# A linear-attention layer with a two-matrix feed-forward: wider idle products, and the last output tile copied and sent by columns

## The chip, the cores and the metric

One of the cores of a Trainium2 chip runs the whole program. The metric is the device time in microseconds (us) of one execution; lower is better. The engines are TensorE (PE, its weight loads shown apart as PEld), VectorE (DVE), ScalarE (ACT), GpSimd (POOL) and SyncE (SP). SP and ACT issue the DMAs; their issuing instructions are shown as SPq and ACTq, and their DMAs appear as queue q1 (SP) and q10 (ACT).

## What is computed

```python
def _attn_ref(r, k, v, w, u):                # all (4, 8, 768, 48), u (8, 48)
    for t in range(S):
        cur = np.einsum('bhd,bhe->bhde', u[None] * kt, vt)
        y[:, :, t] = np.einsum('bhd,bhde->bhe', rt, state + cur)
        state = wt[:, :, :, None] * state + np.einsum('bhd,bhe->bhde', kt, vt)

def _moe_ref(x, w_in, w_out, alpha):          # x (3072, 384), w_in (384, 2048), w_out (2048, 384)
    h = x @ w_in
    g = np.maximum(h, 0.0) + alpha * np.minimum(h, 0.0)
    return (g @ w_out).astype(np.float32)
```

The output of the attention, laid out as 3072 tokens of 384 features, is the `x` of the second function. Everything is float32.

## The kernel before

**Tiles and groups.** Time is cut into chunks of 64 steps; a chunk of two batches is one attention tile of 128 partitions (`q`, 24 of them). Three such tiles are one group `g` of 384 tokens (`GS = 3`, `GT = 384`; eight groups). For each group the feed-forward runs over 16 slices of the hidden size (`j`): `moe_up` makes 128 hidden features of 384 tokens in a PSUM bank (L684), ACT and DVE apply the slope (L689, L691) and split the result in two float32r parts (L695, L696), and `moe_down` adds the products with `w_out` to three PSUM tiles `op0` to `op2` (L709), one for each 128 tokens. Group 0 works on plain float32 (`wf`, `pos`); later groups on pairs of float32r parts. `moe_out` copies `op0` to `op2` to SBUF and sends them to the output.

**What sets the order.** All work is first written as operations of a planner (`Plan`), with an engine, a planned duration, what it reads and writes, and a due time; a simulated run of the plan puts them in order, and the program is emitted in that order. Each engine executes its own list in order. The plan's numbers are not times of the chip.

**Idle products of PE.** `warm()` is a 128x128 block of the constant 1e-18 that POOL sets at the start (L315, in a tile of the ring `os`). PE first runs `MADE = 12` products of that block with itself (`wm`, L738), into a PSUM bank that nobody reads. While the program is emitted, wherever the plan leaves PE idle for more than `FILL_MIN`, before the first use of `op2`, further such products are put in (L834), as many as fit at `FILL = 0.24` us each, into `op2`. There are 17 of them, in seven places: 2, 3, 3, 3, 2, 1 and 3. A plain float32 product shows as two MATMUL records and two weight loads in the trace. So L738 has 24 records and L834 has 34.

**The last output.** In the last group ACT copies `op0` (L726) and DVE copies `op1` and `op2` (L723), 384 columns each. Every tile holds 64 rows of each of two batches, and goes out in two DMAs (L731) of 64 partitions by 384 columns (1,536 bytes a row): in the last group the first half of the partitions is issued by SP and the second by ACT. Behind its last DMA each engine loads a flag (L992) and branches on it (L993): the other branch, for inputs of another range, is not taken. SP then waits for every outstanding DMA, and some closing semaphore work ends the program.

Of the kernel before, what the change touches and what calls it, by code (L numbers as in the profile page):

```python
# [8 lines left out]
F32 = mybir.dt.float32  # L9
# [9 lines left out]
B, H, S, D = 4, 8, 768, 48  # L19
DM, DF = 384, 2048  # L20
P = 128
NP = H // 2
T = 64
NC = S // T
NB = B // 2
NQ = NC * NB
# [6 lines left out]
GS = 3  # L33
NG = NQ // GS
GT = GS * P
# [9 lines left out]
STEP = 3.12  # L45
# [16 lines left out]
MADE = 12  # L62
# [4 lines left out]
FILL, FILL_MIN = 0.24, 0.35  # L67
# [32 lines left out]
class Plan:  # L100
# [6 lines left out]
    def op(self, eng, dur, fn, r=(), w=(), lat=0.1, due=None, lock=False, kind=None, after=0.0):  # L107

        o = Op()
        o.eng, o.dur, o.lat, o.fn, o.due, o.lock, o.kind = eng, dur, lat, fn, due, lock, kind  # L110
        o.after = after
        o.n, o.deps, o.succ, o.takes, o.uses, o.start = len(self.ops), {}, [], [], [], None
        self.ops.append(o)
        o.keys = {*r, *w}
        keys = [(k if isinstance(k, tuple) else (k, None), k in w) for k in list(dict.fromkeys([*r, *w]))]
        for key, written in keys:
            t = key[0]
            if isinstance(t, Tensor) and t not in o.uses:
                o.uses.append(t)
                t.users += 1  # L120
                if t.first is None:
                    t.first = o.n
                    o.takes.append(t)
                else:
                    o.deps[t.first] = True
            if key in self.writer:
                o.deps[self.writer[key]] = True
            if written:
                for x in self.readers.get(key, ()):
                    o.deps.setdefault(x, False)  # L130
        for key, written in keys:
            if written:
                self.writer[key], self.readers[key] = o.n, []
            else:
                self.readers.setdefault(key, []).append(o.n)
        o.deps.pop(o.n, None)
        return o
# [100 lines left out]
def fast_path(tc, alpha_n, flag, dmaj, nat, u, ud, wts, alpha, out):  # L238
# [4 lines left out]
    nc = tc.nc  # L243
    plan = Plan()
    op = plan.op
# [4 lines left out]
    with tc.tile_pool(name="const", bufs=1) as const, tc.tile_pool(name="psum", bufs=1, space=PSUM) as psum, \  # L250
            tc.tile_pool(name="wts", bufs=1) as wpool:
        def ring(name, shape, n, dtype=F32, pool=const, ordered=True):
            return Ring([pool.tile(shape, dtype, name=f"{name}_{i}") for i in range(n)], ordered)
# [3 lines left out]
        ops_ = [psum.tile([P, DM], F32, name=f"op{s}") for s in range(GS)]  # L257
# [42 lines left out]
        r_gl = ring("gl", [P, GT], 3, F32R)  # L300
# [4 lines left out]
        tmp, sp = Tensor(r_os), Tensor(r_os)  # L305

        def warm():
            return tmp.ap[:, 2 * P:]

        def spread():  # L310
            return pairs(sp.ap, P)
# [24 lines left out]
        def c_spread():  # L336
# [5 lines left out]
           r=["ident"], w=["twin"])  # L342
# [23 lines left out]
        due_att, due_step, now = {}, [], 0.0  # L366
# [112 lines left out]
        def scores(q):  # L479

            c, b = divmod(q, NB)
            kr, nv, at = ready[q]
            yb[q], opened[q] = (Tensor(bank), Tensor(bank)), set()

            def products():
                if c > 0:
                    carried(q, kr, 1, False)
                for p in range(NP):  # L490
                    for o in range(2):
                        for i in range(2):
                            mm(q, 1 - o, FULL[i], slice(YC + p * T, YC + (p + 1) * T), True, lhsT=kr.ap[FULL[o], 0, p, FULL[i]],
                               rhs=kr.ap[FULL[o], 1, p, FULL[i]])

            def rest():
                for o in range(2):
                    op("DVE", 0.34, lambda o=o: nc.vector.copy_predicated(
                        out=at.ap[:, o], mask=mask.unsqueeze(1).broadcast_to([P, NP, T]),
                        data=pairs(yb[q][1 - o].ap[:, YC:YC + NP * T], T)),  # L500
                       r=["mask", yb[q][1 - o]], w=[(at, o)])
            return products, [(kr, 0), (kr, 1), *([("St", b, 0), ("St", b, 1)] if c > 0 else [])], yb[q], rest
# [213 lines left out]
        def moe_out(n, g):  # L716
            for s in range(GS):
                q = g * GS + s
                c, b = divmod(q, NB)
                os_ = Tensor(r_os if q < NQ - 1 else r_pos)  # L720
                last = g == NG - 1
                if s == 1 or last and s == GS - 1:
                    op("DVE", 0.47, lambda s=s, os_=os_: nc.vector.tensor_copy(out=os_.ap, in_=ops_[s]),  # L723
                       r=[("op", s)], w=[os_], due=due_step[n] + STEP)
                else:
                    op("ACT", 0.37, lambda s=s, os_=os_: nc.scalar.copy(out=os_.ap, in_=ops_[s]),  # L726
                       r=[("op", s)], w=[os_], due=due_step[n] + STEP)
                for i in range(2):
                    t0 = (2 * b + i) * S + c * T
                    eng, queue = ("ACT", nc.scalar) if last and i else ("SP", nc.sync)  # L730
                    op(eng, 0.5, lambda t0=t0, i=i, os_=os_, queue=queue: queue.dma_start(out=out[t0:t0 + T, :], in_=os_.ap[FULL[i], :]),  # L731
                       r=[os_], w=[("out", q, i)], lat=0.3, due=due_step[n] + STEP + 8.0)


        def wm():
            t = wm_t.ap
            for _ in range(MADE):
                nc.tensor.matmul(t[:, 0:P], lhsT=warm(), rhs=warm(), start=True, stop=True)  # L738
        wm_t = Tensor(bank)
        op("PE", 4.4, wm, r=[(tmp, "warm")], w=[wm_t], kind="MM", due=0.0)  # L740
        for q in range(NQ):
# [2 lines left out]
        for q in range(NQ):  # L744
            if q == 0 or q not in joined:
# [3 lines left out]
                products, r, w, rest = scores(q)  # L749
# [34 lines left out]
        for i in range(NQ // 2):  # L784
# [3 lines left out]
            for h in range(2):  # L788
                op("ACT", 0.72, lambda i=i, v=v, h=h: nc.scalar.activation(
                    out=v()[:, h], in_=v()[:, h], func=AF.Relu, bias=m_one[:, 0:1],  # L790
                    accum_out=wv_all[:, 2 * i + h:2 * i + h + 1]), r=["m_one"], w=[(raw, h), ("wv", 2 * i + h)])

        for j in range(NF):
            raw = Tensor(r_raw)
            check_load(NQ // 2 + j, wts.bitcast(I32)[j], lambda raw=raw: raw.ap.rearrange("p f t -> p (f t)"))
            for h in range(2):
# [3 lines left out]
                    out=w1(), in_=w1(), func=AF.Relu, scale=-1.0, bias=tiny[:, 0:1],  # L800
                    accum_out=wt_all[:, 2 * j + h:2 * j + h + 1]), r=["tiny"], w=[(raw, h), ("wt", 2 * j + h)])

        def at_most_zero(i, src, keys, how):
# [6 lines left out]
            out=pc_all, in0=pc_all, scalar1=PMIN, scalar2=None, op0=ALU.is_gt),  # L810
           w=[("pc", q) for q in range(NQ)], due=late)
        op("DVE", 0.2, lambda: nc.vector.tensor_reduce(out=ok4[:, 0:1], in_=pc_all, axis=AX.XY, op=ALU.min),
           r=[("pc", q) for q in range(NQ)], w=[("ok4", 0)])
# [4 lines left out]
           r=[("ok4", i) for i in range(4)], w=[("ok4", 4)])  # L818
        fp = Tensor(bank)
        op("PE", 0.2, lambda: nc.tensor.matmul(fp.ap[0:1, 0:1], lhsT=ok4[:, 4:5], rhs=ones, start=True, stop=True),  # L820
           r=[("ok4", 4), "ones"], w=[fp], kind="MM", due=late + 4.0)
# [6 lines left out]
        at, use = 0.0, next(o.start for o in order if ("op", GS - 1) in o.keys)  # L828
        with tc.manual_schedule():
            for o in order:  # L830
                if o.eng == "PE":
                    if 0 < at < o.start - FILL_MIN and o.start < use:
                        for _ in range(int((o.start - at - FILL_MIN) / FILL) + 1):
                            nc.tensor.matmul(ops_[GS - 1][:, 0:P], lhsT=warm(), rhs=warm(), start=True, stop=True)  # L834
                    at = o.start + o.dur
                if o is hint:
                    tc.mark_branch_hint_location("general", "LikelyTaken", [mybir.EngineType.SP, mybir.EngineType.Activation])
                o.fn()
# [216 lines left out]
```

## Time and profile before

| | us |
|---|---|
| three runs | 507.19, 507.32, 510.42 |
| median | 507.32 |
| the profiled execution | 509.57 |
| its span, first to last instruction | 507.8 |

The profile describes one execution. Busy shares are averages over a head (to about 82 us, in which the weights are prepared) and a long body of products. Because each engine has an order of its own, the reading goes by the chain of work that ended last, and at the end by the DMAs, which that chain doesn't show. A DMA's row gives when it is issued, and the DMA view how long it takes from issue to landing.

### The profile page before, as it was taken

The page shows a single profiled execution, that of the slowest core. Times are in us where ns is not written, and L with a number is a line of the kernel's source. Part 1 is how long each engine was busy: PE and PEld are TensorE (multiplying, and loading weights), DVE is VectorE, ACT ScalarE, POOL GpSimd, SP SyncE. Part 2 cuts the span into 40 slices and gives each one's busy share as a digit, 9 for nine tenths or more (in the row PEclk, how much of TensorE's full clock was granted, in tenths as well). Part 3 has the DMA queues.
Part 4 walks back from the last instruction along what each step waited for, and adds up shares of the span by engine and source line. Part 5 has one row for each costly group of instructions (what it writes and reads, how often), then busy time and mean ns, then how long its engine had stood idle before and what let it go on. Part 6 is the DMA issues. An engine that isn't in the chain of part 4 may idle for free.

```text
span 507.8 us, 13048 instructions
## 1 busy us (share of the span) xinstructions
PE 496.1 (98%) x5406; PEld 458.7 (90%) x5406; DVE 337.6 (66%) x602; ACT 291.5 (57%) x746; POOL 74.0 (15%) x103
## 2 busy tenths in 40 slices
PE   8999998999999999999999999999999999999995
PEld 8876664689999999999999999999999999999995
DVE  6899997999987564956478474855556353443332
ACT  4866574563363535456585765776677676553331
POOL 2010333233014010222014020030000000000000
PEclk9999998999999999999999999999999999999999
DMA  8648884561163311736157461756445441210001
GB/s 300 234 179 294 298 297 166 181 185 43 43 178 86 104 52 65 185 99 224 60 171 215 126 207 46 258 168 205 146 140 196 139 159 63 71 44 21 1 3 52
DMA packets 27107, 72.40 MB, mean 143 GB/s; under 512 B 3680, under 2 KB 8224, under 8 KB 27040
## 3 DMA queue, kind: packets, MB, share of 16 engines
q1 hardware_dynamic: 26656, 71.19, 43.5%
q8 instruction: 44, 0.72, 0.6%
q10 hardware_dynamic: 384, 0.30, 0.2%
q14 instruction: 23, 0.19, 0.1%
HBM read 64.70 MB, written 4.72 MB: 137 GB/s over the span
## 4 chain that ended last, share of the span: by engine, by line
PE 70%; DVE 11%; DMA 9%; ACT 5%; issue 3%; SPq 2%; ACTq 0%; DVEq 0%
PE bank L684 31%; PE op L709 30%; DMA raw<-in_wts_dram 6%; PE bank L467 6%; DMA kr<-in_dmaj_dram 2%; ACT at L448 1%; DVE cx L650 1%; DVE wf L654 1%; DVE suf L410 1%; DVE pos L691 1%; DVE kr L419 1%; PE bank L513 1%; DVE gl L696 1%; DVE kr L422 1%; SPq L621 1%
## 5 line engine op out<-in xcount | busy, mean ns | idle before, releaser
L684 PE MATMUL bank<-x,wh 128*128 128x384 f32 x672 | 191.3, 338 | 0.0
L689 ACT ACTIVATE pos<-bank,alpha_n 128x384 f32<-128x384 f32 (+1 forms) x133 | 75.4, 569 | 104.5 <-PE bank L684 102.3
L691 DVE SCALAR_TENSOR_TENSOR pos<-bank,pos 128x384 f32<-128x384 f32 (+1 forms) x133 | 71.6, 538 | 89.4 <-ACT pos L689 89.2
L684 PEld LDWEIGHTS bank<-x,wh 128*128 128x128 f32 x672 | 123.0, 188 | 1.2
L709 PE MATMUL op<-wh,gl 128*128 128x384 f32 x336 | 113.0, 336 | 1.0 <-DVE gl L696 0.7
L709 PE MATMUL op<-wh,gh 128*128 128x384 f32 x336 | 113.1, 337 | 0.0
L709 PE MATMUL op<-wl,gh 128*128 128x384 f32 x336 | 112.5, 335 | 0.0
L684 PE MATMUL bank<-x,wl 128*128 128x384 f32 x336 | 112.4, 335 | 0.0
L696 DVE TENSOR_TENSOR gl<-pos,gh 128x384 fp32r<-128x384 f32 x112 | 67.1, 599 | 54.8 <-ACT gh L695 54.8
L695 ACT CAST gh<-pos 128x384 fp32r<-128x384 f32 x112 | 57.5, 514 | 53.5 <-DVE pos L691 52.7
L709 PEld LDWEIGHTS op<-wh,gl 128*128 128x128 f32 x336 | 63.1, 188 | 2.9 <-DVE gl L696 2.9
L709 PEld LDWEIGHTS op<-wh,gh 128*128 128x128 f32 x336 | 63.1, 188 | 0.1
L684 PEld LDWEIGHTS bank<-x,wl 128*128 128x128 f32 x336 | 63.1, 188 | 0.0
L709 PEld LDWEIGHTS op<-wl,gh 128*128 128x128 f32 x336 | 63.1, 188 | 0.0
L458 POOL TENSOR_TENSOR St<-St,pc_all 128x192 f32<-128x192 f32 x44 | 23.8, 562 | 248.7 <-DVE St L611 209.8
L448 ACT ACTIVATE at<-twin,cd 128x64 f32<-128x64 f32 x192 | 52.6, 343 | 0.9 <-PE bank L467 0.7
L684 PE MATMUL bank<-xw,wf 128*128 128x384 f32 (+2 forms) x126 | 35.9, 425 | 2.3 <-DVE wf L654 2.3
L709 PE MATMUL op<-wf,pos 128*128 128x384 f32 x96 | 35.4, 499 | 0.0
L410 DVE TENSOR_TENSOR_SCAN suf<-wd,low 128x528 f32<-128x528 f32 x24 | 30.9, 1287 | 3.9 <-DMA wd<-in_dmaj_dram 3.9
L416 DVE TENSOR_TENSOR_SCAN wd<-wd,low 128x528 f32<-128x528 f32 x24 | 33.4, 1391 | 0.1
L684 PEld LDWEIGHTS bank<-xw,wf 128*128 128x128 f32 x126 | 20.9, 193 | 13.1 <-DVE wf L654 3.1
L440 POOL TENSOR_TENSOR rk<-rk,u_bc 128x384 f32<-128x384 f32 x19 | 20.3, 1069 | 84.1 <-DMA rk<-in_nat_dram 49.3
(81 smaller groups left out, 530.0 us busy)
## 6 DMA issues: line engine op xcount, KB each, us to landing
raw<-in_wts_dram SPq DMA_DIRECT2D x32, 768.0 KB, 5.1
kr<-in_dmaj_dram SPq DMA_DIRECT2D x24, 512.0 KB, 3.9
rk<-in_nat_dram SPq DMA_DIRECT2D x19, 384.0 KB, 3.7
wd<-in_dmaj_dram SPq DMA_DIRECT2D x24, 264.0 KB, 2.8
raw<-in_dmaj_dram SPq DMA_DIRECT2D x12, 528.0 KB, 4.2
nv<-in_nat_dram SPq DMA_DIRECT2D x24, 256.0 KB, 4.9
out_dram<-os SPq DMA_DIRECT2D x44, 96.0 KB, 2.2
x<-x SPq DMA_DIRECT2D x28, 72.0 KB, 4.6
```

Source lines behind the costliest of these rows:

```text
L410: op("DVE", 1.17, lambda: nc.vector.tensor_tensor_scan(out=suf.ap[:, ::-1], data0=w.ap[:, ::-1], data1=low[:, ::-1], initial=0.0, op0=ALU. ...
L416: op("DVE", 1.17, lambda: nc.vector.tensor_tensor_scan(out=w.ap, data0=w.ap, data1=low, initial=0.0, op0=ALU.mult, op1=ALU.max), r=["low"] ...
L440: op("POOL", 1.0, lambda i=i: nc.gpsimd.tensor_tensor(out=rk.ap[:, 0:HD], in0=rk.ap[:, 0:HD], in1=u_bc if i == 0 else rk.ap[:, HD:], op=AL ...
L448: nc.scalar.activation(out=at.ap[:, o, p, :], in_=twin, func=AF.Copy, scale=cd.ap[:, o * NP + p:o * NP + p + 1])
L458: op("POOL", 0.6, lambda i=i: nc.gpsimd.tensor_tensor(out=St[b][:, i, :, 0:D], in0=St[b][:, i, :, 0:D], in1=pc_all[:, q, i::2].unsqueeze(2 ...
L467: nc.tensor.matmul(yb[q][i].ap[rows, cols], start=(i, rows.start) not in opened[q], stop=stop, skip_group_check=True, **kw)
L684: nc.tensor.matmul(hp.ap[:, ts], lhsT=a, rhs=b[:, k, ts], start=(i == 0), stop=(i == m - 1))
L689: op("ACT", 0.15 + 0.33 * share, lambda: nc.scalar.activation(out=pos.ap[:, ts], in_=hp.ap[:, ts], func=AF.Relu, scale=alpha_n[:, j:j + 1] ...
L691: op("DVE", 0.07 + 0.4 * share, lambda: nc.vector.scalar_tensor_tensor(out=pos.ap[:, ts], in0=hp.ap[:, ts], scalar=0.0, in1=pos.ap[:, ts], ...
L695: op("ACT", 0.43, lambda: nc.scalar.copy(out=gh.ap, in_=pos.ap), r=[pos], w=[gh])
L696: op("DVE", 0.47, lambda: nc.vector.tensor_tensor(out=gl.ap, in0=pos.ap, in1=gh.ap.bitcast(F32), op=ALU.subtract), r=[pos, gh], w=[gl], lo ...
L709: nc.tensor.matmul(ops_[s], lhsT=a.ap[:, ts], rhs=w, start=(j == 0 and i == 0), stop=(j == NF - 1 and i == len(todo) - 1))
```

## The change

The constant block is now 128x384 and lies in the third tile of the ring `gl` (a float32r tile read as float32), which the feed-forward writes much later. The 12 first products become 4 with 384 moving columns; the filling products of one place are joined, up to three in one (128, 256 or 384 columns). The last attention tile's output (`q == NQ - 1`, the `op2` of the last group) is copied in two halves of 192 columns, one by DVE, one by ACT, and each half goes out in one DMA of both batches' rows: SP sends DVE's half, ACT its own.

```diff
         def warm():
-            return tmp.ap[:, 2 * P:]
+            return r_gl.tiles[2].bitcast(F32)
@@ moe_out
-                if s == 1 or last and s == GS - 1:
+                if q == NQ - 1:
+                    rows = out.rearrange("(n t) f -> n t f", t=S)[2 * b:2 * b + 2, c * T:(c + 1) * T]
+                    for i, (eng, copy, queue) in enumerate((("DVE", nc.vector.tensor_copy, nc.sync), ("ACT", nc.scalar.copy, nc.scalar))):
+                        fs = slice(i * DM // 2, (i + 1) * DM // 2)
+                        op(eng, 0.27, lambda s=s, os_=os_, fs=fs, copy=copy: copy(out=os_.ap[:, fs], in_=ops_[s][:, fs]),
+                           r=[("op", s)], w=[(os_, i)], due=due_step[n] + STEP)
+                        op("SP" if i == 0 else "ACT", 0.5, lambda os_=os_, fs=fs, rows=rows, queue=queue: queue.dma_start(
+                            out=rows[:, :, fs], in_=os_.ap[:, fs]),
+                           r=[(os_, i)], w=[("out", q, i)], lat=0.3, due=due_step[n] + STEP + 8.0)
+                    continue
+                if s == 1:
@@ wm
-            for _ in range(MADE):
-                nc.tensor.matmul(t[:, 0:P], lhsT=warm(), rhs=warm(), start=True, stop=True)
+            for _ in range(MADE * P // GT):
+                nc.tensor.matmul(t[:, 0:GT], lhsT=warm()[:, 0:P], rhs=warm(), start=True, stop=True)
@@ emitting the order
-                        for _ in range(int((o.start - at - FILL_MIN) / FILL) + 1):
-                            nc.tensor.matmul(ops_[GS - 1][:, 0:P], lhsT=warm(), rhs=warm(), start=True, stop=True)
+                        n = int((o.start - at - FILL_MIN) / FILL) + 1
+                        for i in range(0, n, GS):
+                            f = min(GS, n - i) * P
+                            nc.tensor.matmul(ops_[GS - 1][:, 0:f], lhsT=warm()[:, 0:P], rhs=warm()[:, 0:f], start=True, stop=True)
```

On TensorE, this is the start of the list (`bank` is a PSUM bank, `op_74` the tile `op2`, `gl_143` and `os_144` the constant block; a place with 3 filling products reads x3 before):

```order
-L1050 UNCONDITIONAL_BRANCH
-L738 MATMUL bank_75<-os_144 128x128 x12
-L834 MATMUL op_74<-os_144 128x128 x2
+L1062 UNCONDITIONAL_BRANCH
+L748 MATMUL bank_75<-gl_143 128x384 x4
+L846 MATMUL op_74<-gl_143 128x256
 L433 MATMUL bank_76<-u_dm,rk_121 128x2 x4
-L834 MATMUL op_74<-os_144 128x128 x3
+L846 MATMUL op_74<-gl_143 128x384
 L513 MATMUL bank_77<-ident,kr_118 128x112 x4
 L467 MATMUL bank_79<-kr_118 64x64 x2
```

The idle products keep their places and are fewer and wider; no other product moves.

On ScalarE, the end of the list before (`op_72` is `op0`, `os` and `pos` the SBUF tiles that are sent):

```order
L689 ACTIVATE pos_135<-bank_76,alpha_n 128x384
L695 CAST gh_138<-pos_135 128x384
L726 COPY os_144<-op_72 128x384
L731 DMA out_dram<-os_144 64x384
L731 DMA out_dram<-os_145 64x384
L731 DMA out_dram<-pos_136 64x384
L992 TENSOR_LOAD flag
```

and of the changed kernel:

```order
L689 ACTIVATE pos_135<-bank_76,alpha_n 128x384
L695 CAST gh_138<-pos_135 128x384
L736 COPY os_144<-op_72 128x384
L741 DMA out_dram<-os_144 64x384
L741 DMA out_dram<-os_145 64x384
L726 COPY pos_136<-op_74 128x192
L728 DMA out_dram<-pos_136 2x64x192
L1004 TENSOR_LOAD flag
```

ACT's new copy stands behind its two earlier DMA issues, and the last DMA writes 2 x 64 x 192 elements where it wrote 64 x 384. On SyncE the end of the list keeps its order, with the same new form of the last DMA:

```order
L741 DMA out_dram<-os_144 64x384
L741 DMA out_dram<-os_145 64x384
L728 DMA out_dram<-pos_136 2x64x192
L1005 COMPARE_AND_BRANCH
```

Before, the third of these rows read `out_dram<-pos_136 64x384`.

## Rows read from the trace of the kernel before

**Rows 1.** The page: busy time of each engine, share of the span, instructions.
```profile
PE 496.1 (98%) x5406; PEld 458.7 (90%) x5406; DVE 337.6 (66%) x602; ACT 291.5 (57%) x746; POOL 74.0 (15%) x103
```

**Rows 2.** Chain that ended last, 60 to 130 us: start, duration, what.
```profile
82.15 3.23 PE bank L684 x6
...
88.37 1.95 PE bank L684 x6
```

**Rows 3.** The same chain in the first 36 us.
```profile
3.28 8.59 DMA raw<-in_wts_dram
...
21.01 0.70 PE op L709 x2
...
30.37 0.87 PE op L834 x6
```

**Rows 4.** The same chain, its last pieces.
```profile
496.94 5.22 PE op L709 x30
...
502.19 0.56 DVE pos L723
```

**Rows 5.** Timeline of the last DMA issues: start, duration, queue, line, what.
```profile
501.13 1.65 SPq L731 DMA_DIRECT2D out_dram<-os  x2
501.13 1.63 ACTq L731 DMA_DIRECT2D out_dram<-os  x2
...
502.81 0.61 ACTq L731 DMA_DIRECT2D out_dram<-pos  x1
502.87 0.81 SPq L731 DMA_DIRECT2D out_dram<-pos  x1
```

**Rows 6.** DMAs, 498 to 508 us: packets, MB, share; size, us to landing.
```profile
q10 hardware_dynamic: 240, 0.30, 11.9%
q1 hardware_dynamic: 240, 0.30, 10.6%
...
out_dram<-pos ACTq DMA_DIRECT2D x1, 96.0 KB, 3.2
out_dram<-pos SPq DMA_DIRECT2D x1, 96.0 KB, 3.4
```

**Rows 7.** The first products (L738): ns min/median/max, first and last start (us).
```profile
L738 PE MATMUL bank<-os x24: 275/421/581, 1.1 to 5.4; 128*128 128x128 f32 x24
```

**Rows 8.** The filling products (L834), the same columns.
```profile
L834 PE MATMUL op<-os x34: 275/275/377, 5.6 to 31.0; 128*128 128x128 f32 x34
```

**Rows 9.** Stretches: PE, PEld, DVE, ACT, POOL busy, granted clock, DMA share, GB/s.
```profile
81.00:82.00 1.00, 0.00 (x0) 0.00 (x0) 1.00 (x2) 1.00 (x6) 0.00 (x0) 1.00 0.04 15
80.00:100.00 20.00, 17.85 (x174) 11.12 (x175) 18.98 (x28) 12.06 (x30) 4.86 (x4) 0.91 0.54 176
```

**Rows 10.** Timeline of the head: start, duration of two settings by POOL.
```profile
0.81 0.20 POOL L315 MEMSET os<- 128x128 f32 x1 [0.29 <-POOLq L1042]
...
3.52 0.42 POOL L334 MEMSET os<- 128x384 f32 x1
```

**Rows 11.** ACT's copies of 192 columns from PSUM: ns min/median/max, starts.
```profile
L589 ACT COPY xw<-bank x6: 319/320/325, 17.1 to 32.6; 128x192 f32<-128x192 f32 x6
```

**Rows 12.** DVE's operations on 192 columns from PSUM, the same columns.
```profile
L611 DVE TENSOR_TENSOR St<-bank,St x40: 307/349/358, 36.0 to 408.0; 128x192 f32<-128x192 f32 x40
```

**Rows 13.** DMAs, 420 to 428 us: one load of 128 rows (columns as rows 6).
```profile
q1 hardware_dynamic: 144, 0.79, 27.0%
```

**Rows 14.** DMAs, 453.5 to 459 us: six outputs of SP; rate in 40 slices.
```profile
GB/s 0 0 0 0 56 223 201 179 56 101 212 201 168 34 0 0 0 0 0 67 223 190 179 56 101 235 190 156 34 45 179 235 190 67 89 223 201 168 34 0
...
q1 hardware_dynamic: 480, 0.59, 49.8%
issues: line engine op xcount, KB each, median us to landing
out_dram<-os SPq DMA_DIRECT2D x6, 96.0 KB, 2.2
```

**Rows 15.** A stretch of loading with all DMA engines busy (columns as rows 9).
```profile
12.50:13.00 0.50, 0.50 (x49) 0.50 (x41) 0.50 (x2) 0.47 (x3) 0.00 (x0) 1.00 1.12 452
```

**Rows 16.** DMAs, 0 to 5 us: ACT's one DMA of 128 32-byte rows.
```profile
q10 hardware_dynamic: 144, 0.00, 1.4%
```

## The prediction

> **What bounds the kernel now.** I read the page first, for the busiest engine: PE, 98% of the span [rows 1]. That alone says little about an edit that touches only the head and the last five microseconds, so I went on to the chain of work that ended last. From 82.15 us on the chain is PE without a gap [rows 2], until the last product of `op2` ends and DVE copies it [rows 4]. Whatever delays PE after 82 us is paid in full. Before that the chain changes hands: it waits for a load of weights until 11.87 us (3.28 + 8.59), then goes through PE, later DVE and again a load [rows 3]. The chain view stops at DVE's copy (502.19 + 0.56 = 502.75 us), but the span lasts until 507.8. The timeline of the issues and the DMA view fill these five microseconds: the last two DMAs are issued at 502.81 (ACT) and 502.87 (SP) and take 3.2 and 3.4 us to land [rows 5, 6], so the last lands at 502.87 + 3.4 = 506.27, and 1.5 us of closing semaphore work follow. The reader is to see that the copy is only the first half microsecond of this tail, and that SP and ACT are both still busy with earlier issues until 501.13 + 1.65 = 502.78 and 501.13 + 1.63 = 502.76 [rows 5].
>
> **The head: wider products.** POOL's setting grows from 128 to 384 columns, 0.20 to about 0.42 us [rows 10], so PE starts 0.2 us later. The first products: the record of 128 columns takes 421 ns in the median against 275 ns for the same shape a little later [rows 7, 8], so PE is at the lower of its two clock levels (1.2 of 2.4 GHz) for most of this block, although the clock column reads 1.00 there. A pair of 384-column records in a stream takes 0.70 us at the full level [rows 3], and six take 3.23 us where most run at the lower level, against 1.95 us [rows 2]. Eight records therefore cost between 8 x 0.32 = 2.6 and, at twice that, 5.2 us; the 24 narrow ones ran from 1.1 to 5.7. The block ends at the earliest 2 us sooner, at the latest 0.8 us later. Either way it is covered: the chain waits for the load until 11.87 us [rows 3]. Without that cover the cost would be the 0.8.
>
> Fillings: three narrow products cost 0.87 us on the chain at 30.37 us, and one of 384 columns costs a pair's 0.70 [rows 3]. Two and one narrow products against 256 and 128 columns are nearly equal. Of the four triple places only this one is on the chain; the others end before the load. That is -0.17 us, and as the chain passes through another engine's work and one more load before 82 us, which need not all move with it, I pass on about half: **-0.1**. The bounds are -0.2 (all of it arrives) and +0.2 (none does, and POOL's longer setting is felt in full).
>
> Could the wider products change the clock where it counts? In this execution the granted clock is 0.91 over 80 to 100 us, after PE had stood idle (81 to 82 us show no product) [rows 9]; 20 x 0.09 = 1.8 us are lost there, on a stretch where PE is the chain. But no filling is emitted after the first use of `op2`, so that idle time stays as it is. I take 0 for the clock. The 1.8 us also explain most of the distance between the profiled execution (509.57) and the median (507.32). The sum below is made on the profiled span and then set on the median: the same difference, with such a loss in neither.
>
> **The tail: the copies.** DVE's half takes about 0.35 us instead of 0.56 [rows 4, 12], so it ends at 502.54. SP gains nothing from that, because it is busy until 502.78 [rows 5]: it issues at 502.87 as before. ACT's half stands behind its two issues in its list, so it starts at about 502.79, takes 0.32 [rows 11] and lets ACT issue at about 503.17, 0.36 later than now. Behind it on ACT stand only the flag load and the branch, for which nobody waits. So the split copy itself is worth between -0.1 and +0.36 us.
>
> **The tail: the form of the last DMAs.** Each still moves 96 KB, as 128 rows of 768 bytes instead of 64 of 1,536. But the output is now written as 2 x 64 x 192: the outermost count is 2. So far every DMA's outermost count has been 16, 64 or 128. The completions show that each ran on 16 DMA engines: one load of 128 rows makes 144 packets [rows 13], six outputs of 64 rows make 480, that is 80 each [rows 14]; the rest beyond the rows is 16 every time, one completion for each engine. If a DMA is dealt out over the engines by its outermost count, the last two run on two engines, and the same two. No row decides this; I hold it likelier than not because the outermost count is all that the earlier DMAs have in common.
>
> The Trainium skill, "DMA: Bandwidth & Descriptors", section "Why a DMA increments its semaphore by 16 and not by 1", says just this: the number of engines is the largest one up to 16 that divides the slowest dimension, not of size one, of both sides (here 2 and 128, hence 2), and it is the lowest-numbered engines that are used. It speaks against this change. This trace agrees for its 16s and has no smaller case.
>
> Price on two engines. All engines together reach 452 GB/s in a full stretch [rows 15], 28 GB/s each. The two halves are 2 x 98,304 bytes: 196,608 / 56.5 GB/s = 3.5 us. Each packet also has a fixed part: 144 tiny ones take 1.4% of 16 x 5 us, 7.8 ns each [rows 16], and 128 per engine make 1.0 us. Sum **4.5 us**, lower bound 3.5. Upper bound: outputs on all engines reach only 235 GB/s at their best [rows 14], 14.7 each, and 196,608 / 29.4 GB/s = 6.7 us. I take 4.5, since two engines alone get in nobody's way, which many writers at once may do.
>
> Around it lies the fixed part of a DMA. Alone, an output lands after 2.2 us [rows 14], of which some 0.5 is its data (98,304 bytes at 179 to 235 GB/s): 1.7 us. Of the last 3.4 us the same leaves 2.9, because four others were in front. I take 2.0, nearer to the lone one, since part of the 2.9 was waiting for the twin that now comes later. So the last byte lands at 502.87 + 2.0 + 4.5 = 509.37 instead of 506.27: **+3.1 us**. Ends: 1.7 + 3.5 gives 508.07 (+1.8), 2.9 + 4.5 gives 510.27 (+4.0). The closing work moves along.
>
> Sum: -0.1 + 3.1 = **+3.0 us**. On the profiled execution that is 509.57 + 3.0 = 512.6; on the median 507.32 + 3.0 = **510.3**.
>
> **The rivals.**
> *Sixteen engines.* The last DMAs are dealt out as ever, by rows. For it: every DMA so far was. Then SP lands as before or a little sooner, with its twin no longer in front, and ACT, issued at 503.17, lands after about 3.2 us at 506.4. That is +0.1, with the head 0: about 507.3, between 506.8 and 507.6. This is the case that is not slower. It decides if each last DMA shows 144 packets.
> *Two engines at the slow rate.* 6.7 us of data instead of 4.5: 502.87 + 2.0 + 6.7 = 511.6 (+5.3), with the 2.9 even +6.2. That is 512.5 to 513.4, slower by over 1%. For it: outputs have not gone faster than 14.7 GB/s per engine here. Against: these were many engines at once.
> *A gain from the clock.* Wider products keep the clock up better and the 1.8 us at 83 us vanish in executions that have them. Against: the idle stretch there isn't touched, and the last filling product starts 50 us earlier, at 31.0 [rows 8]. It gives 507 to 508 at sixteen engines, no more.
>
> **How the numbers follow.** Two engines at about full rate 0.65, sixteen engines 0.22, two engines at the slow rate 0.08, the rest 0.05. The forecast is the likeliest, 510.3; its own range is 509.0 to 511.2 (+1.8 and +4.0, less the 0.1), and 512.1 if the loss of clock falls into the middle run. The range over the cases is 506.9 to 512.1, since sixteen engines hold more than may be left out. Some 1% (5.1 us, from 502.2 to 512.4) is what a measurement of this kernel can tell from no change. Over 1% slower is the slow rate and part of a clock loss on top of two engines, 0.10; over 1% faster has no mechanism, 0.01; the rest, 0.89, is within 1%.
>
> **What would show it.** Two engines: in the last stretch q1 and q10 show 290 packets (two outputs of 80 and one of 128 + 2) instead of 240, the last two landings grow to about 6 us, and the DMA share stays near 2 of 16 for four microseconds. Sixteen: 304 packets and landings of 3 us. ACT's copy should start at about 502.8 and ACT's issue follow at 503.2; if the copy starts at 502.2, ACT's earlier issues do not hold it. PE's first block should end between 3.7 and 6.5 us, and the chain should still pass through the load until 11.9. The prediction is wrong if the landings stay near 3 us, or if the body after 82 us moves by more than the clock's 1.8 us.

## The result, and the profile after

The changed kernel takes 512.19 us (median of 511.79, 512.11, 512.27 and 517.64); the kernel before, run beside it, 507.59. The ratio on record is 1.0124, 95% interval 1.0079 to 1.0168; the two medians alone stand at 1.0091. The forecast was 510.3 with a range to 512.1: the time lies 0.1 us beyond the range, and between the medians the loss is 4.6 us where 3.0 were forecast. A second series (`e10` below) gave 512.51 against 507.46, ratio 1.0110 [1.0072, 1.0149].

The profiled execution of the changed kernel took 512.27 us, its span is 510.5. Lines shift: L738 is now L748, L834 is L846, L723 and L726 are L733 and L736, L731 is L741; L726 is now the copy by columns and L728 its DMA. The page still shows PE busy almost all the time, with 36 fewer records than in [rows 1]:

```profile
PE 495.4 (97%) x5370; PEld 455.6 (89%) x5370; DVE 336.3 (66%) x602; ACT 291.8 (57%) x747; POOL 78.2 (15%) x103
```

**The tail.** The chain of the last 28 us, whose last pieces answer to [rows 4], and under it the timeline of the last issues, which answers to [rows 5] (start, duration, what):

```profile
496.19 4.69 PE op L709 x27
500.88 0.02 issue
500.91 0.56 DVE os L733
501.46 0.34 DVE pos L726
501.80 0.19 ACTq L741
502.00 0.04 issue
502.04 0.32 ACT pos L726
```

```profile
500.37 1.59 SPq L741 DMA_DIRECT2D out_dram<-os  x2
500.38 1.62 ACTq L741 DMA_DIRECT2D out_dram<-os  x2
...
502.05 0.63 SPq L728 DMA_DIRECT2D out_dram<-pos  x1
502.39 1.10 ACTq L728 DMA_DIRECT2D out_dram<-pos  x1
```

DVE's half ends at 501.79, but SP is busy with its earlier issues until 501.96 and issues at 502.05. ACT's half waits for ACT's own issues and starts at 502.04; its DMA is issued 0.34 us behind SP's. Now the DMA view of the last stretch, which answers to [rows 6] (the rate in 40 slices of 0.325 us, then packets, MB and share of each queue):

```profile
GB/s 0 0 0 0 0 0 0 50 0 0 38 208 293 66 161 203 269 72 61 40 28 40 45 38 51 47 47 45 45 47 47 45 30 0 0 0 0 0 0 0
DMA packets 586, 0.66 MB, mean 50 GB/s; under 512 B 68, under 2 KB 580, under 8 KB 580
## 3 DMA queue, kind: packets, MB, share of 16 engines
q1 hardware_dynamic: 290, 0.30, 10.1%
q10 hardware_dynamic: 290, 0.30, 6.7%
```

There are 290 packets in each queue, 80 + 80 + 130: the last output has 128 rows and two completions. From 503.5 us on the rate is 72, 61 and then 28 to 51 GB/s, until the packets of the two halves end at 508.5. SP's half is through at about 506.9 and ACT's at 508.5; SP sees the last completion at 509.03, and 1.5 us of closing work end the span at 510.54. From the end of PE's last product to the end of the span the trace of before has 5.7 us (502.15 to 507.84), that of the change 9.15 (501.39 to 510.54): **+3.45 us**.

**The head.** The chain of the first 36 us, which answers to [rows 3]:

```profile
0.93 2.84 DMA wd<-in_dmaj_dram
...
9.45 0.59 DVE rk L406
10.08 1.05 PE bank L433 x8
11.13 0.75 PE op L846 x2
...
29.15 0.84 PE op L846 x2
```

It no longer goes through the load of raw weights until 11.87; it runs through DVE to 10.04 and then PE. The filling product at 29.15 takes 0.84 us where three narrow ones took 0.87. The first block, by its line's own view (ns min/median/max, first and last start):

```profile
L748 PE MATMUL bank<-gl x8: 486/847/1008, 1.3 to 5.5; 128*128 128x384 f32 x8
```

It ends at 6.0 us, between the 3.7 and 6.5 forecast, and nobody waits for it.

**The body.** PE's waits from 92 to 490 us, first before, then after (engine, line, released by: us in total, times, longest):

```profile
PE op L709 <- DVE gl L696: 0.7, 2, 0.5
```

```profile
PE op L709 <- ACT gh L695: 1.4, 1, 1.4
PE bank L684 <- issue: 0.4, 1, 0.4
PE op L709 <- DVE gl L696: 0.2, 1, 0.2
```

The second has a wait of 1.4 us at 330.3, and behind it the clock goes down for 3.4 us. This row covers that place (columns as in [rows 9]):

```profile
330.00:334.00 4.00, 2.42 (x9) 1.87 (x8) 1.12 (x2) 3.10 (x8) 2.43 (x3) 0.84 0.53 219
```

To compare stretches of unequal start I measured the body in every trace in one way: from the start of PE's 4,300th product record before the end to that of the 20th. It is 402.92 us before and 405.15 after, **+2.2 us**. The head up to there is 95.60 before and 92.61 after, because this one execution of before had stood idle for 2.3 us at 79.8 and then lost clock [rows 9]. So the spans add up: -3.0 + 2.2 + 3.5 = +2.7 (507.84 to 510.54). The head's -3.0 belongs to the two executions; the tail is the forecast mechanism; the 2.2 us in the body were not forecast at all.

### The profile page after: what moved, and what is told of

The parts are those of the page before. It is cut to its first block, busy times and chain, and to the rows that moved or that the text cites. A ratio compares the mean times of both kernels' runs of the same rounds, so it can differ in the third digit from the quotient of the medians.

```text
span 510.5 us, 12977 instructions
## 1 busy us (share of the span) xinstructions
PE 495.4 (97%) x5370; PEld 455.6 (89%) x5370; DVE 336.3 (66%) x602; ACT 291.8 (57%) x747; POOL 78.2 (15%) x103
## 4 chain that ended last, share of the span: by engine, by line
PE 86%; DVE 5%; DMA 4%; issue 1%; ACT 1%; SPq 0%; ACTq 0%; DVEq 0%
PE bank L684 39%; PE op L709 36%; PE bank L467 8%; DMA raw<-in_wts_dram 4%; PE bank L513 1%; DVE suf L410 1%; PE bank L576 1%; DVE wf L654 1%; DMA wd<-in_dmaj_dram 1%; PE bank L433 1%; DVE wl L666 1%; PE op L846 0%; SPq L621 0%; DVE kr L419 0%; DVE cx L650 0%
## 5 line engine op out<-in xcount | busy, mean ns | idle before, releaser
L696 DVE TENSOR_TENSOR gl<-pos,gh 128x384 fp32r<-128x384 f32 x112 | 66.1, 590 | 54.4 <-ACT gh L695 54.4
L440 POOL TENSOR_TENSOR rk<-rk,u_bc 128x384 f32<-128x384 f32 x19 | 24.3, 1280 | 80.5 <-DMA rk<-in_nat_dram 54.1
```

Source lines behind the costliest of these rows:

```text
L440: op("POOL", 1.0, lambda i=i: nc.gpsimd.tensor_tensor(out=rk.ap[:, 0:HD], in0=rk.ap[:, 0:HD], in1=u_bc if i == 0 else rk.ap[:, HD:], op=AL ...
L696: op("DVE", 0.47, lambda: nc.vector.tensor_tensor(out=gl.ap, in0=pos.ap, in1=gh.ap.bitcast(F32), op=ALU.subtract), r=[pos, gh], w=[gl], lo ...
```

## The experiments

Single executions of one and the same program scatter by several us here (28 of the kernel before in one series took 503.1 to 511.3), so the kernels below were timed in 6 to 12 runs each beside the kernel before; only `e12` was run once.

**Head alone, tail alone, and two forms of the tail.** `e1`: the change with the old `moe_out`. `e2`: before with the new `moe_out`. In `e3` the change sends each half by batches, in `e4` it copies by columns but sends full rows:

```diff
 # e3
-    out=rows[:, :, fs], in_=os_.ap[:, fs]
+    for e in range(2): out=rows[e, :, fs], in_=os_.ap[FULL[e], fs]      # 64x192
 # e4
+    SP: out=rows[0], in_=os_.ap[FULL[0], :]; ACT: rows[1], FULL[1]      # 64x384, after both copies
```

> The wider first and filling products alone, with the last output as before. Theory A (all of the loss is the two-engine form of the last two DMAs): the ratio to before is 1.000, within 0.001, and the tail from the end of the last product to the end of the span stays at about 5.6 us as before. Rival B (the wider products cost time in the head, a later or lost clock): the ratio is 1.004 or more, with the chain in the first 36 us later than before or with more stretches below a clock of 1.00. Rival C (the wider products gain in the head, as the profile of the changed kernel has PE's product of line L576 at 14.7 us where it was at 16.0): 0.997 to 0.998.

> The column halves of the last output alone, with the narrow products of before. Theory A: the whole loss, +4 us or a ratio of 1.008, with two last landings of 5 to 7 us and 130 packets for each of the two last DMAs. Rival B: clearly less than the changed kernel's 1.012, 1.004 to 1.006, with the rest found in the wider products alone.

> The changed kernel, but each column half is sent by two DMAs of one batch each (64 rows of 768 bytes, outermost count 64). Copies, queues, bytes and row length are those of the changed kernel; only the outermost count differs, and there are two DMAs more. Theory A (the outermost count of 2 confines each DMA to two engines): 80 packets for each of the four DMAs, landings of 3 to 4 us, and a ratio to before of 1.000 to 1.002. Rival D (rows of 768 bytes are dear whatever the engines): landings of 5 us or more and 1.006 or above.

> The changed kernel, with the column halves copied by DVE and ACT, but sent as before, 64 rows of 1,536 bytes by SP and 64 by ACT, each after both copies. Theory A: 1.000 (0.999 to 1.001), with ACT's copy starting only when ACT has issued its DMA of the tile before, so that the copy by halves gains nothing. Rival E (the copy by halves itself costs or gains): more than 0.3 us away from before, visible in the time from the last product's end to the last two issues.

| | median, us | before beside it | ratio, 95% interval | last product to end of span |
|---|---|---|---|---|
| e1 | 509.20 | 506.33 | 1.0063 [1.0037, 1.0089] | 5.1 |
| e2 | 510.72 | 506.33 | 1.0072 [1.0041, 1.0103] | 9.2 |
| e3 | 509.99 | 506.33 | 1.0077 [1.0048, 1.0107] | 6.7 |
| e4 | 510.02 | 506.33 | 1.0054 [1.0024, 1.0084] | 6.8 |

The last column, from one trace each, tells the tail's story: with the two-row DMA 9.2 us, without it 5.1 to 6.8. In the 13 traces with the old last output it takes 5.0 to 5.9 us, 5.4 in the mean, and in the three with the two-row DMA 9.0 to 9.2, so the +3.45 of the profiled pair is +3.7 in the mean. The DMA view of `e3` (last 14 us; at the end the landing) shows the form undone, two outputs of 64 + 16 packets for the one of 130:

```profile
q1 hardware_dynamic: 320, 0.30, 9.8%
q10 hardware_dynamic: 320, 0.30, 7.5%
...
out_dram<-pos SPq DMA_DIRECT2D x2, 48.0 KB, 3.5
out_dram<-pos ACTq DMA_DIRECT2D x2, 48.0 KB, 3.4
```

So 768-byte rows are not what costs, though `e3`'s ratio alone would fit that rival: its landings stay at 3.5 us. About 1 us over the old tail remains in `e3` and `e4`. Both still have ACT's copy behind its issues; `e3` issues two DMAs more, `e4` waits for both copies. But `e1` is a miss: the wider products, which I had put at nothing, cost 2.9 us. That is not in the tail. `e3` and `e4`, which have the wider products too and were expected at 1.000 to 1.002 and 1.000, miss with it.

**The parts of the head.** `e5` is the program of before under a second label; `e6` moves only the constant block to the ring `gl`; `e7` widens only the first products, `e8` only the filling ones.

```diff
 # e6
-    return tmp.ap[:, 2 * P:]
+    return r_gl.tiles[2].bitcast(F32)[:, 0:P]
 # e7: block of 128x384 there, and the first products 128x384 (4); the filling ones stay 128x128
 # e8: block of 128x384 there, and the filling products joined; the first ones stay 128x128 (12)
```

> The kernel before, unchanged, timed as if it were another kernel: the comparison of a program with itself. If the ratio is 1.000 within its interval, the 1.005 to 1.006 of the wider products alone is a cost of these products. If it is 1.004 or more, a share of every ratio here is not the edit's, but comes from how one loaded program runs against another, and the differences between edited kernels count, not those to before.

> Narrow products as before; only the constant block lies in the third tile of the ring gl instead of the ring os, so that nothing of the head but an address and the waits on that tile differ. If the place of the block costs (a wait of the first L696 that writes this tile, or of ACT's L579 that no longer waits for PE), 1.003 or more; if the width costs, 1.000.

> Only the first products are wide (4 of 384 columns), the fillings narrow. If the first block costs (PE starts 0.2 us later, the clock's rise comes later), 1.005 as with both; if the fillings cost, 1.000.

> Only the fillings are wide (up to 384 columns), the first 12 products narrow, with the setting of 384 columns by POOL. If the fillings cost, 1.005; if the first block costs, 1.000. If this one, the wide first block and the narrow block in the other ring all come out alike at 1.004 to 1.006, none of them is the cause, and what they share is that they are not the program of before.

Medians 507.80, 507.29, 507.71 and 507.33 us against 506.79; ratios 1.0012 [0.9985, 1.0040], 1.0010 [0.9991, 1.0029], 1.0014 [0.9993, 1.0034] and 1.0009 [0.9986, 1.0032]. Neither kind of wider products, nor the place of the block, stands apart from the same program run again.

**Again, and two more forms of the tail.** `e9` is `e1`'s program, `e10` that of the change. `e11` is `e3`'s tail with narrow products. `e12` is the kernel before with each last output cut into 24 and 40 rows, to see how a DMA is dealt out.

```diff
 # e12
-    out=out[t0:t0 + T, :]
+    for r0, r1 in ((0, 24), (24, T)): out=out[t0 + r0:t0 + r1, :]
```

> Both kinds of wider products once more, the last output as before: the same program as the first experiment, which gave 1.006, while each kind alone gave 1.001 on another chip. If the 1.006 belongs to the program, it comes again (1.004 to 1.008). If it belonged to how that load or that chip ran, it is 1.001, within 0.999 to 1.003.

> The changed kernel once more, beside the wider products alone on the same chip. The two differ only in the last output. Theory A (two engines): 3.5 us above the wider products alone, as the tail after the last product grew from 5.7 to 9.2 us in the profiles; against before 1.007 to 1.009 if the wider products cost nothing, 1.012 if they cost 0.005.

> Narrow products as before; the last tile copied by column halves, each half sent by two DMAs of one batch (outermost count 64). Against the column halves alone in the changed kernel's form (1.007) only the outermost count differs. Theory A: 1.001 to 1.003, 80 packets for each of the last four DMAs and a tail of 6.5 to 7 us in place of 9.2, of which the part above 5.7 is the two more DMAs and ACT's copy behind its issues. Rival D (short rows): 1.006 or more.

> The kernel before, with each of the last two DMAs of 64 rows cut in one of 24 and one of 40 rows, to see how the number of engines follows from the outermost count. If it is the largest number up to 16 that divides the count: 12 engines for 24 rows and 10 for 40, so that each queue shows 24 + 12 + 40 + 10 = 86 packets for its two. If every DMA with 16 rows or more is dealt out on 16: 24 + 16 + 40 + 16 = 96.

`e9`: 509.20 us against 507.46, ratio 1.0036 [1.0001, 1.0071]. `e10`: 512.51, 1.0110 [1.0072, 1.0149]. The two differ only in the tail, by 3.3 us. `e9`'s ratio falls between its two expected ranges and decides nothing. `e11`: 508.90, 1.0037 [1.0009, 1.0065], a little over the 1.001 to 1.003 expected, its last product 7.0 us before the end. `e12` took 507.09 in its one run, and its DMA view shows:

```profile
q1 hardware_dynamic: 246, 0.30, 8.4%
q10 hardware_dynamic: 246, 0.30, 6.4%
```

246 packets are 160 for the two earlier outputs and 86 for the two pieces: 24 + 40 rows and 22 completions. 12 + 10 is what the Trainium skill, "DMA: Bandwidth & Descriptors", section "Why a DMA increments its semaphore by 16 and not by 1", makes of them: the largest number up to 16 that divides 24, and the one for 40. The packet count gives only the sum of 22; the semaphore events of the trace give the two parts: behind one early event on each of the four semaphores, 12 arrive for the 24 rows and 10 for the 40. In the changed kernel 2 arrive for each half, and 16 for each of the last outputs before, so the runs agree with the Trainium skill for 2, 10, 12 and 16 engines.

In `e9`'s trace a loss in the body can be followed. The timeline at 208 to 216 us, without the rows between (in brackets: idle time before, and what ended it):

```profile
209.16 0.69 DVE L419 TENSOR_TENSOR kr<-kr,suf 128x512 f32<-128x512 f32 x1 [1.31 <-DMA kr<-in_dmaj_dram]
...
210.35 0.52 ACT L695 CAST gh<-pos 128x384 fp32r<-128x384 f32 x1 [1.92 <-DVE pos L691]
...
211.68 1.19 POOL L440 TENSOR_TENSOR rk<-rk,u_bc 128x384 f32<-128x384 f32 x1 [6.33 <-DMA rk<-in_nat_dram]
...
212.00 1.28 DVE L696 TENSOR_TENSOR gl<-pos,gh 128x384 fp32r<-128x384 f32 x1
...
213.34 0.44 PE L709 MATMUL op<-wh,gl 128*128 128x384 f32 x1 [1.25 <-DVE gl L696]
```

The inputs of the next group land late (`kr` 6.6 us behind its issue, against 5.0 in `e15`, which has no such wait); DVE stands still for 1.31 us; the feed-forward's operations queue behind it on DVE; L696 then falls beside POOL's L440, where it takes 1.28 us instead of the 0.53 of a lone one; and PE waits 1.25 us. That meeting of L696 and L440 is not the difference by itself: every trace has five to eight L696 of more than 1 us, those without a wait too. The waits of over 1 us in the bodies of `e3`, `e4` and `e10` that I followed, at this group and the one before, have the same form.

**Both kinds together, each alone, and before, side by side.** Whether `e1` and `e9` had shown the products or the chip on which they ran was open, since `e5` to `e8` ran on another. `e13` to `e16` repeat them on a third:

> The wider warming products and the wider filling products together, with the last output as before. If the two together cost time ahead of the tail: 2.5 to 3 us above the program of before, as in the two earlier runs of this program. If that belonged to the chip of those runs: within 1 us of the program of before under its second label. The tail after the last product, 5 to 6 us, is that of before under both theories.

> Only the warming products wider. If only the two kinds together cost time, or if the earlier difference belonged to the chip: within 1 us of the program of before under its second label, as on the other chip (0.9 us above). If the warming products alone cost it on the chip of the earlier runs: 2 us or more above.

> Only the filling products wider. If only the two kinds together cost time, or if the earlier difference belonged to the chip: within 1 us of the program of before under its second label, as on the other chip (0.5 us above). If the filling products alone cost it on the chip of the earlier runs: 2 us or more above.

> The program of before under a second label, run in the same places of the order as the three others. Ratio 1.000 within its interval; what it stands apart from the runs of before, up to 0.6 us so far, is what the place in the order is worth and is taken off the other three.

| | median, us | ratio to 507.05 | 95% interval |
|---|---|---|---|
| e13, both wide | 508.93 | 1.0030 | 1.0004 to 1.0057 |
| e14, first wide | 506.18 | 0.9988 | 0.9960 to 1.0016 |
| e15, filling wide | 506.52 | 0.9996 | 0.9967 to 1.0025 |
| e16, before | 506.49 | 0.9983 | 0.9958 to 1.0009 |

Both kinds together stand 2.4 us above the program of before under its second label (2.5 to 3 were expected), each alone at it. So it is the two together, on two chips and in three series. Added effects would not do that. What the two together change, and neither alone as far, is the number of PE's instructions: 5,406 records before, 5,390 with wide first products, 5,386 with wide filling ones, 5,370 with both. The trace shows code as packets of its own, 44 of 16 KB in queue q8, and with 5,370 records some of them come elsewhere; that they are PE's is read from their places, which follow PE's records (below). This is the DMA view of five quiet us ahead of a group's loads, before (366 to 371 us) and, at the same products, after (366 to 371):

```profile
DMA packets 1, 0.02 MB, mean 3 GB/s; under 512 B 0, under 2 KB 0, under 8 KB 0
...
q8 instruction: 1, 0.02, 1.4%
```

```profile
DMA packets 0, 0.00 MB, mean 0 GB/s; under 512 B 0, under 2 KB 0, under 8 KB 0
```

After, that packet comes in the next five us, at 372.4, 0.4 us ahead of the first load, and runs into the loads:

```profile
q1 hardware_dynamic: 301, 0.92, 60.2%
q8 instruction: 1, 0.02, 1.6%
```

In the traces this packet starts with 1,246 or 1,247 PE records still to come in the eight kernels of 5,406 records (`e17` below is one), with 1,232 to 1,237 in the four with one kind wide, and with 1,150 to 1,162 in the eight of 5,370. So its place goes by the number of records, and not in proportion: 16 or 20 fewer hardly move it, which fits the two kinds costing time only together. But this one place can't be the whole cause: before, the next packet, at 375.4, falls among the same loads.

**Number against width.** `e17` is `e1` with 18 tiny products behind the first block, so that there are 5,406 records again; `e18` is the wide filling products with 4 narrow first ones, 5,370 records.

```diff
 # e17
+    for _ in range(18):
+        nc.tensor.matmul(t[:, 0:2], lhsT=warm()[:, 0:P], rhs=warm()[:, 0:2], start=True, stop=True)
 # e18
-    for _ in range(MADE):
+    for _ in range(MADE * P // GT):
         nc.tensor.matmul(t[:, 0:P], lhsT=warm()[:, 0:P], rhs=warm()[:, 0:P], start=True, stop=True)
```

> Both kinds of idle products wide, the last output as before, and behind the first block 18 more products of 2 columns, so that PE has as many products in all (5,406 records) as the kernel before instead of 5,370. They take some 2 us in the time until 10 us, in which the chain waits for other things. If the number of PE instructions costs the 2 us: back at the time of before, within 1 us; the code packets of q8 between 330 and 400 us come at the places of before (one near 365 us, not 372), PE's wait without a releaser near 380 us is gone, and its idle time from 100 to 490 us falls from the 1.5 to 3.4 us of the traces with both kinds wide to under 1.2. If the width of both costs it: 2 us above before, as without the added products.

> Wide filling products, and 4 first products of 128 columns instead of 12: as many PE instructions as with both kinds wide (5,370 records), but the first products are narrow. If the number of instructions costs the 2 us: 1.5 to 2.5 us above before, code packets at the places seen with both kinds wide, and the wait without a releaser near 380 us is there. If the width of both kinds costs it: as with the wide filling products alone, within 1 us of before. The shorter first block can leave PE at the lower clock for longer at the start; that would show before 70 us and is taken off.

As whole kernels both missed every expectation: 513.27 and 513.00 us against 507.02, ratios 1.0127 [1.0075, 1.0180] and 1.0132 [1.0071, 1.0192]. The time went in the head, where I had called PE covered. `e17` by stretches (columns as in [rows 9]) shows the clock at its lower level, 1.2 GHz, from 8 to 18 us:

```profile
6.00:8.00 2.00, 2.00 (x20) 2.00 (x19) 2.00 (x3) 0.00 (x0) 0.00 (x0) 0.97 0.98 350
8.00:10.00 2.00, 2.00 (x11) 2.00 (x11) 2.00 (x3) 0.00 (x0) 0.00 (x0) 0.50 1.04 429
10.00:12.00 2.00, 2.00 (x9) 1.82 (x9) 0.21 (x2) 0.00 (x0) 0.00 (x0) 0.50 0.97 383
```

and its chain shows the 36 tiny records, 5.36 us or 0.15 each, during which it fell:

```profile
5.69 5.36 PE bank L740 x36
11.05 1.06 PE op L838 x2
12.12 1.50 PE bank L433 x8
```

In `e18` the short first block leaves PE slow until 20.9 us: L433's eight records take 1.86 us in its chain, against 1.05 after the change.

```profile
6.43 1.86 PE bank L433 x8
8.30 1.49 PE op L836 x2
```

Both kernels so reach the 4,300th record from the end late, at 102.1 and 97.2 us (92.8 in `e16`). Behind it the bodies can be compared, one trace of each kernel:

| PE records | kernels | body, us |
|---|---|---|
| 5,406 | before, e2, e5, e6, e11, e12, e16 | 402.9, 403.0, 400.7, 403.8, 402.8, 402.4, 402.0 |
| 5,406, both kinds wide | e17 | 401.6 |
| 5,390 or 5,386, one kind wide | e7, e14, e8, e15 | 402.1, 401.5, 401.4, 401.2 |
| 5,370, both kinds wide | after, e1, e3, e4, e9, e10, e13 | 405.2, 403.9, 406.9, 405.0, 404.7, 405.7, 406.7 |
| 5,370, filling wide | e18 | 403.7 |

The seven of the fourth line have a mean of 405.4, the seven of the first 402.5: 2.9 us. PE's idle time in this stretch accounts for 2.0 of it: 3.0 us in the mean of the fourth line, 1.0 in that of the first. The heads ahead of it have a mean of 92.6 and 93.3 us, so up to the end of the body 2.2 us of the 2.9 are left, in line with the 1.7 to 2.9 of the whole kernels. The third line, with 16 or 20 records fewer, is as short as the first. `e17` keeps both kinds wide and has the number back: its body is as short as any, and its waits from 92 to 490 us are only these:

```profile
PE op L709 <- DVE gl L696: 0.3, 1, 0.3
```

Its code packets are where they are before (372 to 377 us, ahead of the loads, since `e17` is 6 us late):

```profile
DMA packets 1, 0.02 MB, mean 3 GB/s; under 512 B 0, under 2 KB 0, under 8 KB 0
...
q8 instruction: 1, 0.02, 1.1%
```

So in this one trace the width does not cost the body its time. A rival remains: `e17` enters the body 9 us late, and its loads may have gained by that. Against it, the heads of before, `e7` and `e18` are 3 to 5 us late too, and their bodies of 402.9, 402.1 and 403.7 us are not shorter for it; a head 9 us late without the added products was not run. `e18` speaks less clearly: its code packets stand as after the change, and it has waits of 0.9 and 0.5 us at the same two products as `e13`, but 403.7 us is also what the slowest kernel of the first line took (403.8, `e6`). The wait without a releaser near 380 us, expected of it, was absent. That the body goes with the number of PE's instructions is therefore well supported by the set of traces, and that the code comes at other places is shown. Of the 34 code packets in each body, 20 to 23 overlap data packets of q1 in the kernels of 5,406, 5,390 and 5,386 records, and 24 to 28 in those of 5,370. But how a code packet among the loads turns into a late load was not followed: no row shows one packet delaying another. That step stays open.

## Why the prediction was wrong, point by point

*The tail's mechanism* was right, the case given 0.65. Two engines, 290 packets a queue, SP gaining nothing from the faster DVE copy, and ACT's copy behind its own issues (0.34 us later, forecast 0.36) all came as worked out. *Its size* was a little low: +3.45 against +3.1. The transfer of the two halves was put at 4.5 us, as 27 ns per row from a full engine's rate and 7.8 ns fixed, 35 ns for each of 128 rows. It measured 5.1 us, 40 ns a row. In the last 3 us the rate is 45 to 47 GB/s, 23 per engine, which is 33 ns a row; the first 2 us went slower. The fixed part of 2.0 us came out at 1.9 (509.03, where the last completion is seen, less 502.05 and 5.1).

*The body* was the step that failed. The sum has -0.1 for the head, 0 for the clock and 3.1 for the tail, and puts what lies between them at nothing, with no reason but that "From 82.15 us on the chain is PE without a gap". That was read from a chain that ends at 130 us [rows 2]. Behind it the same view of before goes through loads as well, among them these two (start, duration, what):

```profile
262.77 6.12 DMA kr<-in_dmaj_dram
326.93 5.14 DMA raw<-in_wts_dram
```

So the body of before hung in part on the time at which loads land, with under 0.5 us of PE idle at any of them, and a later load could lengthen it. The head's own parts are small: the wide filling product on the chain saved 0.03 us, not 0.17, and the first block was covered. But I counted the products that the edit removes as time, and not as instructions that stand ahead of all of PE's later code. With 36 records fewer, the body of the traces is 2.9 us longer in the mean, and whole kernels with both kinds wide are 2.9, 1.7 and 1.9 us slower than before (`e1`, `e9`, `e13`). The prediction named this case only as what would make it wrong, "if the body after 82 us moves by more than the clock's 1.8 us". It did, by 2.2 in the profiled executions.

*The clock* was put at 0. That holds for the place I looked at: the row of 80 to 100 us has 0.91 before and 1.00 after, by chance of the executions, and the loss at 333 us follows a wait of PE, not the products. But the head's cover was overrated: `e17` and `e18` show that a PE at the lower level there costs 4 to 9 us up to the 4,300th record from the end.

*The chain through the load until 11.9* did not come: the load landed at 10.6 us. It landed at 10.8 in `e2` with narrow products too, so the edit isn't the reason.

*The sum:* 3.4 for the tail and some 2 for the number of instructions make 5.4, against a measured 4.6 and 5.05. The differences are within the scatter of the runs. Whether the loss is over 1%, which had a chance of 0.10, depends on the reading: 0.9% and 1.0% between the medians of the two series, 1.24% and 1.10% by the ratios on record. That the time ended only 0.1 us outside the range is no merit of the sum: its tail and its body were both too low.

## What to carry to other kernels

Write the outermost dimension of a DMA as a multiple of 16 rows, above all where it is the last one: the same 2 x 96 KB in halves with an outermost count of 2 had a tail of 9.2 us, and sent with a count of 64 (`e3`) one of 6.7, and nothing hides the difference. An edit that removes instructions from the head of a long unrolled engine program can move the later loads of that engine's code, as the packets of q8 moved here; time an identical program under a second label, and one with the number of instructions restored, before believing in a difference of 2 us. Compare stretches between fixed products rather than whole spans, since a disturbed head (here by tiny products at a falling clock) can hide what the body tells.

## What the runs showed of the hardware

- The number of engines that a DMA ran on was the largest one up to 16 that divides its outermost count: 2 for 2, 12 for 24, 10 for 40, 16 for 64, by the completions in the packet counts and the semaphore events.
- Of two DMAs from two queues on the same two engines, SP's data ran from 503.5 to 506.9 us and ACT's, issued 0.34 us later, from 505.5 to 508.5, so that they shared 1.4 us and ran one after the other for the rest.
- DVE's 128x384 operation L696 took 0.53 us alone and 1.28 beside a POOL operation of the same shape (`e9`).
- Records of 2 columns took 0.15 us each, and the granted clock fell from 1.00 to 0.50 while they ran; it stayed there for 10 us.
- The granted-clock column reads 1.00 in `e18` at 6 to 12 us, where L433's records take 1.86 us for 1.05: before the first recorded change of the clock, at 20.9 us there, the column did not tell the level.
